# Linear attention on one core: rows 256 to 511 of x transposed by the DMA crossbar instead of TensorE, with the first crossbar transpose issued earlier

## The chip, the core and the metric

The kernel runs on one core of a Trainium2 chip. The core has five engines that run their own instruction streams: TensorE (PE in the profile, with PEld for its weight loads), VectorE (DVE), ScalarE (ACT), GpSimd (POOL) and SyncE (SP). DMAs are issued by an engine's stream, here by SP and ACT, and run on 16 DMA engines that all queues share. The metric is the device time of one execution in microseconds.

## What is computed

One block of linear attention, B=1, S=2048 rows, D=640, 32 heads of 20 columns, all in bf16:

```python
qkv = (x @ wqkv).reshape(B, S, 3, H, Dh) ...      # q, k, v
phi = lambda t: jnp.where(t > 0, t + 1, jnp.exp(t)) + 1e-6
pq, pk = phi(q), phi(k)
kv  = einsum("bhsd,bhse->bhde", pk, v);  z = einsum("bhsd->bhd", pk)
num = einsum("bhqd,bhde->bhqe", pq, kv)
den = einsum("bhqd,bhd->bhq", pq, z)[..., None] + 1e-6
out = (num / den) ... @ wo
```

## The kernel before, in words

x is held twice in SBUF: xn with its rows on the partitions (16 tiles of 128 rows), and xT, its transpose, as five chunks of 128 columns of x. A matmul that computes K for a row tile takes the xT columns of that tile as the stationary operand, so a row tile of K cannot start before its part of xT is there.

The stages follow each other on TensorE in this order:

1. Six warming matmuls on a constant (L269).
2. K: for each row tile st, `k_half(st, 0)` and `k_half(st, 1)` (L273, matmul at L278), five chunks each, ten matmuls a tile, 160 in all. The result lies in two PSUM banks, 2*(st%4) and the next. `k_phi(st)` (L287) then makes phi of it: an Exp on ScalarE (L291) and two operations on VectorE (L293, L296), into pk.
3. P = x^T pk (`p_step`, L305), with xn as the stationary operand, in two halves of the columns. Q tiles (`q_tile`, L331) are put between its steps; they read wqp, a permuted copy of wqn that ScalarE makes at the end of the K stage (L259), and xT.
4. The sums of pk (L350), the small per-head products (L408, L432), the denominators (L454), the spreading of their reciprocals by DMA (L471).
5. The output rows (L487), copied out by ScalarE and VectorE (L509, L512) and stored (L497).

**How xT is filled.** The table XCH (L176) cuts the rows into chunks. The first NPE = 4 chunks, of 128 rows each, are transposed on TensorE: `transpose_x(st, b)` (L189) makes five transposes of 128 by 128 (L194) of the tile xn[st] into PSUM bank b, and two VectorE copies (L199) bring them to xT. The other chunks come straight from DRAM through the DMA crossbar: `load_xT` (L182) issues one transposing DMA each (L184) on SP's queue. Before the change those are seven: one of 128 rows (512 to 639), five of 256 rows, and a last one of 128. `xT_keys` (L205) makes a K tile or a Q tile wait for the chunks that it reads.

**What sets the order.** A planner (`Plan.add`) keeps a list of instructions for each engine in the order in which the code adds them, and works out the semaphore waits from reads and writes. The lists are run in order, so a waiting instruction holds up all that stand behind it on its engine. The first DMAs are issued by `load_wk` (L225): on SP x tile 0, then wk chunk 0, wk chunks 2, then 4, then x tile 3; on ACT x tile 1, wk 1, wk 3, then x tile 2. Behind them on SP stand the crossbar transposes, the first with a wait for wk chunk 4 (L186), and then `load_rest` (L244): wqn, the rest of xn in three loads of four tiles each, wv and wo.

The order on TensorE at the start is written out by hand in a string (L537). `t0` is the transpose of row tile 0, and `k12` is chunk 2 of both halves of K for row tile 1:

```python
order = "t0 t1 k00 k01 k10 k11 k02 k12 k03 k13 t2 k04 k14 t3"
...
transpose_x(st, (st + 2) % 4 + 4)
```

So t0 and t1 use PSUM banks 6 and 7, t2 and t3 banks 4 and 5, which are also the banks of K for row tile 2. After the string follow `k_phi(0)`, `k_phi(1)`, and then, from row tile 2 on, the two halves and phi of each tile.

Of the kernel before, what the change touches and what calls it, by code (L numbers as in the profile page):

```python
# [82 lines left out]
def bass_standalone__linear_attn_block__prompt_kernel(nc, x, wqkv, wo, out):  # L83
    B, S, D = x.shape
# [10 lines left out]
    with contextlib.ExitStack() as ctx:  # L95
        es = ctx.enter_context

        def sb(name, cols, dt=BF16):
            return es(nc.sbuf_tensor(name, [128, cols], dt))

        xT = sb("xT", NC_ * S)
        xn = sb("xn", NT * D)
        wk = sb("wk", NC_ * D)
# [41 lines left out]
        def pool_const():  # L145
# [26 lines left out]
                     0 if lo else DH - 1, 1 if lo else -1, "bm")  # L172


        NPE = 4
        XCH = [(128 * t, 128 * t + 128) for t in range(NPE + 1)] + [  # L176
            (a, min(a + 256, S)) for a in range(128 * NPE + 128, S, 256)]

        def xch_of(row):
            return next(i for i, (a, b) in enumerate(XCH) if a <= row < b)  # L180

        def load_xT():  # L182
            for i, (a, b) in enumerate(XCH[NPE:]):
                P.add("sp", lambda e, a=a, b=b: e.dma_start_transpose(  # L184
                    xT[:, :].rearrange("p (c s) -> p c s", s=S)[:, :, a:b], x[0, a:b, :]),
                    reads=[("wk", 4)] if i == 0 else [],  # L186
                    writes=[("xT", NPE + i)], dma=True)

        def transpose_x(st, b):  # L189
# [15 lines left out]
        def xT_keys(a, b, cs=range(NC_)):  # L205
            keys = []
            for i, (p, q) in enumerate(XCH):
                if p < b and a < q:
                    keys += [("xT", i)] if i >= NPE else sorted(
                        {("xT", i, 0 if c < 2 else 2) for c in cs})  # L210
            return keys

        def w_cols(dst, lo, hi, col, key, eng):
            P.add(eng, lambda e: e.dma_start(
                dst[:, 0:NC_ * D].rearrange("p (c n) -> p c n", n=D)[:, :, lo:hi],
                wqkv[:, col + lo:col + hi].rearrange("(c p) n -> p c n", p=128)),
                writes=[key], dma=True)

        def load_xn(a, b, eng):
            P.add(eng, lambda e: e.dma_start(  # L220
                xn[:, a * D:b * D].rearrange("p (t n) -> p t n", n=D),
                x[0, 128 * a:128 * b, :].rearrange("(t p) n -> p t n", p=128)),
                writes=[("xn", t) for t in range(a, b)], dma=True)

        def load_wk():  # L225
            tl = mybir.InstLoadActFuncSet(
                name=nc.get_next_instruction_name(),
                act_func_set_id=ACT_TABLE_SET_LN_EXP, ins=[], outs=[])
            P.add("act", lambda e: e.add_instruction(tl), writes=["table"])
            for eng, what in (("sp", "x01 w01 w23 w45 x34"), ("act", "x12 w12 w34 x23")):  # L230
                for k in what.split():
                    a, b = int(k[1]), int(k[2])
                    if k[0] == "x":
                        load_xn(a, b, eng)
                    else:
                        P.add(eng, lambda e, a=a, b=b: e.dma_start(
                            wk[:, a * D:b * D].rearrange("p (c n) -> p c n", n=D),
                            wqkv[128 * a:128 * b, D:2 * D].rearrange("(c p) n -> p c n", p=128)),
                            writes=[("wk", c) for c in range(a, b)], dma=True)
# [3 lines left out]

        def load_rest():  # L244
            w_cols(wqn, 0, D, 0, "wqn", "sp")
            for a, b in ((4, 8), (8, 12), (12, 16)):
                load_xn(a, b, "sp")
            w_cols(wv, 0, D, 2 * D, "wv", "sp")
            P.add("sp", lambda e: e.dma_start(
                wog[0:GW, 0:5 * D].rearrange("p (g n) -> p g n", n=D),  # L250
                wo[0:5 * GW, :].rearrange("(g p) n -> p g n", p=GW)),
                writes=["wog"], dma=True)
            P.add("sp", lambda e: e.dma_start(
                wog[0:gsz[5], 5 * D:6 * D], wo[5 * GW:D, :]), writes=["wog5"], dma=True)
# [12 lines left out]
        def warm(*cols):  # L267
            for n in cols:
                P.add("pe", lambda e, n=n: e.matmul(  # L269
                    bank(4, n), one[:, 0:128], one[:, 0:n], start=True, stop=True),  # L270
                    writes=[("bank", 4)])
# [259 lines left out]

        pool_const()
        load_wk()
        load_xT()
        load_rest()
        warm(512, 512, 512, 512, 512, 512)
        order = "t0 t1 k00 k01 k10 k11 k02 k12 k03 k13 t2 k04 k14 t3"  # L537
        for k in order.split():
            st = int(k[1])
            if k[0] == "t":  # L540
# [131 lines left out]
```

## Time and profile before

| what | us |
|---|---|
| median of 3 runs (lowest, highest) | 101.67 (101.2, 102.3) |
| the profiled execution | 101.73 |
| its span from the first to the last instruction | 100.0 |
| TensorE matmuls busy | 96.8 |
| VectorE busy | 69.2 |
| ScalarE busy | 43.3 |
| GpSimd busy | 3.3 |

The times that follow are counted from the span's start. In rows of a timeline, and of the chain that ended last, the first number is the start and the second the duration, or for several merged instructions the busy time, of the group; a note in brackets says how long the engine sat idle before it and what ended that. A DMA row gives the queue that issued it (SPq, ACTq), the size, and the time from issue to landing. A row of windows gives a stretch of time, its length, the busy time and count of PE, PEld, DVE, ACT and POOL, then the granted TensorE clock, the busy share of the DMA engines and the rate of data that they moved.

### The profile page before, as it was taken

The page shows a single profiled execution, that of the slowest core. Times are in us where ns is not written, and L with a number is a line of the kernel's source. Part 1 is how long each engine was busy: PE and PEld are TensorE (multiplying, and loading weights), DVE is VectorE, ACT ScalarE, POOL GpSimd, SP SyncE. Part 2 cuts the span into 40 slices and gives each one's busy share as a digit, 9 for nine tenths or more (in the row PEclk, how much of TensorE's full clock was granted, in tenths as well). Part 3 has the DMA queues.
Part 4 walks back from the last instruction along what each step waited for, and adds up shares of the span by engine and source line. Part 5 has one row for each costly group of instructions (what it writes and reads, how often), then busy time and mean ns, then how long its engine had stood idle before and what let it go on. Part 6 is the DMA issues. An engine that isn't in the chain of part 4 may idle for free.

```text
span 100.0 us, 1793 instructions
## 1 busy us (share of the span) xinstructions
PE 96.8 (97%) x697; PEld 63.0 (63%) x703; DVE 69.2 (69%) x140; ACT 43.3 (43%) x76; POOL 3.3 (3%) x15
## 2 busy tenths in 40 slices
PE   6999999999999999999999999999999999999992
PEld 2556777777777565656667565756446677777771
DVE  0217988888889379799996445758899759853331
ACT  5005554445697220462132227398954523333322
POOL 6600000000000000000000000000000000000000
PEclk9999999999999999999999999999999999999999
DMA  2963999699999900000000000014440324523333
GB/s 56 308 226 71 185 205 137 132 236 377 371 365 289 191 14 0 0 3 0 7 0 0 0 0 0 25 34 123 120 136 1 117 70 153 213 95 120 131 131 131
DMA packets 17076, 11.93 MB, mean 119 GB/s; under 512 B 8749, under 2 KB 17069, under 8 KB 17069
## 3 DMA queue, kind: packets, MB, share of 16 engines
q1 hardware_dynamic: 16349, 11.14, 42.9%
q10 hardware_dynamic: 720, 0.70, 2.1%
q8 instruction: 5, 0.08, 0.3%
q14 instruction: 2, 0.02, 0.1%
HBM read 5.90 MB, written 2.62 MB: 85 GB/s over the span
## 4 chain that ended last, share of the span: by engine, by line
PE 91%; DVE 4%; ACT 2%; issue 1%
PE ps L278 22%; PE ps L487 22%; PE ps L305 22%; PE ps L331 16%; PE ps L269 3%; DVE pq L344 2%; PE ps L194 2%; PE ps L408 2%; PE ps L454 1%; ACT eq L339 1%; DVE pq L479 1%; PE ps L432 1%; DVE eq L341 1%; ACT w2g L436 1%; DVE osb L512 0%
## 5 line engine op out<-in xcount | busy, mean ns | idle before, releaser
L305 PE MATMUL ps<-pk,xn 128*128 128x320 bf16 x160 | 23.5, 299 | 0.0
L331 PE MATMUL ps<-xT,wqp 128*128 128x512 bf16 x94 | 23.1, 379 | 0.3
L278 PE MATMUL ps<-wk,xT 128*128 128x320 bf16 x160 | 22.8, 302 | 0.0
L487 PE MATMUL ps<-w2p,pq 128*128 128x320 bf16 (+1 forms) x165 | 22.1, 295 | 0.1
L339 ACT ACTIVATE eq<-ps 128x512 bf16<-128x512 f32 x20 | 12.0, 599 | 21.2 <-PE ps L331 20.7
L305 PEld LDWEIGHTS ps<-pk,xn 128*128 128x128 bf16 x160 | 15.6, 98 | 7.4 <-DVE pt L320 0.2
L487 PEld LDWEIGHTS ps<-w2p,pq 128*128 128x128 bf16 x165 | 15.8, 98 | 6.6 <-DVE pq L479 0.6
L278 PEld LDWEIGHTS ps<-wk,xT 128*128 128x128 bf16 x160 | 15.4, 99 | 6.6 <-DMA wk<-in_wqkv_dram 0.4
L291 ACT ACTIVATE ek<-ps 128x640 bf16<-128x640 f32 x16 | 11.2, 704 | 14.7 <-PE ps L278 14.7
L331 PEld LDWEIGHTS ps<-xT,wqp 128*128 128x128 bf16 x100 | 9.7, 97 | 9.0
L344 DVE SCALAR_TENSOR_TENSOR pq<-ps,eq 128x512 bf16<-128x512 f32 x20 | 13.8, 692 | 0.7
L296 DVE SCALAR_TENSOR_TENSOR pk<-ps,ek 128x640 bf16<-128x640 f32 x16 | 13.2, 825 | 0.5
L512 DVE CAST osb<-ps 128x320 bf16<-128x320 f32 (+1 forms) x16 | 7.7, 479 | 8.3 <-PE ps L487 8.2
L509 ACT CAST osb<-ps 128x320 bf16<-128x320 f32 (+1 forms) x17 | 7.0, 417 | 13.4 <-PE ps L487 12.1
L341 DVE TENSOR_SCALAR eq<-eq 128x512 bf16<-128x512 bf16 x20 | 5.8, 292 | 9.8 <-ACT eq L339 9.7
L479 DVE TENSOR_TENSOR pq<-pq,rd 128x512 bf16<-128x512 bf16 x20 | 7.7, 416 | 0.4 <-DMA rd<-rdc 0.4
L293 DVE TENSOR_SCALAR ek<-ek 128x640 bf16<-128x640 bf16 x16 | 5.2, 325 | 2.0 <-ACT ek L291 1.9
L199 DVE COPY xT<-ps 128x256 bf16<-128x256 bf16 (+1 forms) x8 | 2.2, 318 | 6.1 <-PE ps L194 6.1
L350 DVE TENSOR_TENSOR za<-pk 128x1280 f32<-128x1280 bf16 x4 | 5.8, 1481 | 0.0
L350 DVE TENSOR_TENSOR za<-za 128x1280 f32<-128x1280 f32 x3 | 4.4, 1480 | 0.0
L259 ACT COPY wqp<-wqn 128x640 bf16<-128x640 bf16 x5 | 4.3, 939 | 0.0
L436 ACT CAST w2g<-ps 120x640 bf16<-120x640 f32 (+1 forms) x6 | 4.0, 690 | 0.0
(38 smaller groups left out, 33.2 us busy)
## 6 DMA issues: line engine op xcount, KB each, us to landing
out_dram<-osb SPq DMA_DIRECT2D x15, 160.0 KB, 1.8
xn<-in_x_dram SPq DMA_DIRECT2D x3, 640.0 KB, 8.0
wqn<-in_wqkv_dram SPq DMA_DIRECT2D x1, 800.0 KB, 5.6
wv<-in_wqkv_dram SPq DMA_DIRECT2D x1, 800.0 KB, 11.2
wog<-in_wo_dram SPq DMA_DIRECT2D x1, 750.0 KB, 13.5
w2p<-w2g SPq DMA_DIRECT2D x5, 150.0 KB
rd<-rdc SPq DMA_DIRECT2D x8, 64.0 KB, 2.3
wk<-in_wqkv_dram SPq DMA_DIRECT2D x3, 160.0 KB, 4.4
```

Source lines behind the costliest of these rows:

```text
L278: r = e.matmul(bank(b + h, HALF), xT[:, c * S + 128 * st:c * S + 128 * st + 128], wk[:, c * D + HALF * h:c * D + HALF * (h + 1)], start=(c ...
L291: P.add("act", lambda e: e.activation(fold(t[:, :]), two_banks(b), ACTF.Exp), reads=banks + ["table"], writes=[("ek", st % 3)])
L296: P.add("dve", lambda e: e.scalar_tensor_tensor(fold(pk[:, st * D:(st + 1) * D]), two_banks(b), 0.0, fold(t[:, :]), ALU.max, ALU.add), rea ...
L305: r = e.matmul(bank(d, HALF), xn[:, st * D + 128 * d:st * D + 128 * d + 128], pk[:, st * D + HALF * h:st * D + HALF * (h + 1)], start=(st ...
L331: r = e.matmul(bank(b), wqp[:, d * D + 128 * c:d * D + 128 * c + 128], xT[:, d * S + BK * sbk:d * S + BK * (sbk + 1)], start=(d == 0), sto ...
L339: P.add("act", lambda e: e.activation(t[:, :], bank(b), ACTF.Exp), reads=[("bank", b), "table"], writes=[("eq", i)])
L344: P.add("dve", lambda e: e.scalar_tensor_tensor(pq[:, c * S + BK * sbk:c * S + BK * (sbk + 1)], bank(b), 0.0, t[:, :], ALU.max, ALU.add), ...
L350: P.add("dve", lambda e: e.tensor_tensor(d_ap, a, b, ALU.add), reads=ra + rb, writes=[dst])
L479: P.add("dve", lambda e: e.tensor_tensor(v, v, rd[i][:, BK * o:BK * (o + 1)], ALU.mult), reads=[("rd", i, 2 * o), ("rd", i, 2 * o + 1), (" ...
L487: r = e.matmul(bank(b, hi - lo), pq[:, c * S + 128 * st:c * S + 128 * st + 128], w2p[:, c * D + lo:c * D + hi], start=(c == 0), stop=(c == ...
L509: P.add("act", lambda e: e.copy(osb[j][:, lo:hi], bank(b, hi - lo)), reads=[("bank", b)], writes=keys)
L512: P.add("dve", lambda e: e.tensor_copy(osb[j][:, lo:hi], bank(b, hi - lo)), reads=[("bank", b)], writes=keys)
```

## The change

Only row tiles 0 and 1 are still transposed on TensorE. Row tiles 2 and 3 (rows 256 to 511) come by the crossbar, as two chunks of 128 rows; the rows from 512 on are cut into six chunks of 256. There are thus eight transposing DMAs. The first of them waits for x tile 1 and no longer for wk chunk 4. The early loads of x tiles 2 and 3 are taken out; these tiles come with the later loads of xn, which now hold four, five and five tiles. The string of the start loses t2 and t3.

```diff
-        NPE = 4
-        XCH = [(128 * t, 128 * t + 128) for t in range(NPE + 1)] + [
-            (a, min(a + 256, S)) for a in range(128 * NPE + 128, S, 256)]
+        NPE = 2
+        XCH = [(128 * t, 128 * t + 128) for t in range(NPE + 2)] + [
+            (a, min(a + 256, S)) for a in range(128 * NPE + 256, S, 256)]
...
                     xT[:, :].rearrange("p (c s) -> p c s", s=S)[:, :, a:b], x[0, a:b, :]),
-                    reads=[("wk", 4)] if i == 0 else [],
+                    reads=[("xn", 1)] if i == 0 else [],
...
-            for eng, what in (("sp", "x01 w01 w23 w45 x34"), ("act", "x12 w12 w34 x23")):
+            for eng, what in (("sp", "x01 w01 w23 w45"), ("act", "x12 w12 w34")):
...
-            for a, b in ((4, 8), (8, 12), (12, 16)):
+            for a, b in ((2, 6), (6, 11), (11, 16)):
                 load_xn(a, b, "sp")
...
-        order = "t0 t1 k00 k01 k10 k11 k02 k12 k03 k13 t2 k04 k14 t3"
+        order = "t0 t1 k00 k01 k10 k11 k02 k12 k03 k13 k04 k14"
```

## The prediction

> **What bounds the kernel now.** I read the page first, its busy shares and the chain that ended last, then that chain in order of time, then TensorE's timeline of the first 10 us, and last the DMA issues with their landings.
>
> ```profile
> span 100.0 us, 1793 instructions
> PE 96.8 (97%) x697; PEld 63.0 (63%) x703; DVE 69.2 (69%) x140; ACT 43.3 (43%) x76; POOL 3.3 (3%) x15
> ...
> PE 91%; DVE 4%; ACT 2%; issue 1%
> ```
>
> TensorE is busy for nearly the whole span and 91% of the chain, so work taken off it there comes off the time, unless it then waits.
>
> ```profile
> 4.78 2.67 PE ps L278 x16
> 7.45 0.38 PE ps L194 x5
> 7.83 0.54 PE ps L278 x4
> 8.38 0.28 PE ps L194 x5
> 8.66 19.16 PE ps L278 x140
> 27.82 4.75 PE ps L305 x35
> ```
>
> The third and fifth lines from the bottom are t3 and t2; both lie on the chain. Behind them 140 matmuls of K (row tiles 2 to 15) run in one piece into the P stage. 4.75 us for 35 matmuls of 320 columns is 0.136 each, so a row tile of ten takes 1.36.
>
> ```profile
> 4.72 2.73 PE L278 MATMUL ps<-wk,xT 128*128 128x320 bf16 x16
> 7.38 0.45 PE L194 MATMUL ps<-ident,xn 128*128 128x128 bf16 x5
> 7.67 0.71 PE L278 MATMUL ps<-wk,xT 128*128 128x320 bf16 x4
> 8.21 0.44 PE L194 MATMUL ps<-ident,xn 128*128 128x128 bf16 x5
> ...
> 8.49 1.12 PE L278 MATMUL ps<-wk,xT 128*128 128x320 bf16 x6
> ...
> 7.38 0.28 PEld L194 LDWEIGHTS ps<-ident,xn 128*128 128x128 bf16 x5 [0.26 <-DMA xn<-in_x_dram]
> ...
> 9.30 0.11 PEld L278 LDWEIGHTS ps<-wk,xT 128*128 128x128 bf16 x2 [0.30 <-DVE xT L199]
> 7.87 0.55 DVE L199 COPY xT<-ps 128x256 bf16<-128x256 bf16 x2 [2.50 <-PE ps L194]
> 8.70 0.56 DVE L199 COPY xT<-ps 128x256 bf16<-128x256 bf16 x2 [0.27 <-PE ps L194]
> ```
>
> This is the same stretch by TensorE's own records. t2 starts when x tile 2 lands; row tile 2 of K starts at 8.49. Its second half waits at 9.30 for the copies of t3, which hold PSUM bank 5.
>
> **The change, part by part.** *t2 and t3 go.* The 16 matmuls end at 4.72 + 2.73 = 7.45. One takes some 0.30 to drain and the next starts 0.136 after it, so k04 can start at 7.45 - 0.30 + 0.14 = 7.29 if wk chunk 4 is there, and row tile 2 four matmuls later, at 7.83, in place of 8.49: 0.66 us earlier. *The bank 5 stall goes.* The six matmuls from 8.49 take 1.12; without a gap they would take 5 x 0.136 + 0.30 = 0.98. That gives 0.14 more, 0.80 in all. The four VectorE copies (1.1 us) go too; VectorE is 69% busy, so I count them at nothing beyond the stall.
>
> What is late next is the crossbar. Row tiles 2, 3 and 4 are now needed at 7.83, 9.19 and 10.55, and every later tile 1.36 after its neighbour.
>
> ```profile
> 7.13 11.99 SPq L184 DMA_TRANSPOSE xT<-in_x_dram  x7
> 19.17 0.58 SPq L214 DMA_DIRECT2D wqn<-in_wqkv_dram  x1
> ...
> L184 SPq DMA_TRANSPOSE xT<-in_x_dram x1: 1331/1331/1331, 7.1 to 7.1; - x1
> ...
> DMA to landing us min/median/max: 3.0/3.0/3.0
> ...
> L184 SPq DMA_TRANSPOSE xT<-in_x_dram x1: 1372/1372/1372, 8.5 to 8.5; - x1
> ...
> DMA to landing us min/median/max: 4.1/4.1/4.1
> ...
> L184 SPq DMA_TRANSPOSE xT<-in_x_dram x1: 1768/1768/1768, 9.9 to 9.9; - x1
> ...
> DMA to landing us min/median/max: 4.4/4.4/4.4
> ...
> xT<-in_x_dram SPq DMA_TRANSPOSE x1, 6.1
> ```
>
> The four single issues are the first (128 rows), the second and third (256 rows) and the one with the longest landing. SP is held some 1.4 us by an issue at first and 1.7 on the mean (11.99 for 7). Landings are 7.13 + 3.0 = 10.1, then 12.6, then 14.3.
>
> ```profile
> 0.84 0.39 ACTq L220 DMA_DIRECT2D xn<-in_x_dram  x1
> ...
> xn<-in_x_dram ACTq DMA_DIRECT2D x1, 160.0 KB, 2.8
> ...
> 2.67 0.43 SPq L220 DMA_DIRECT2D xn<-in_x_dram  x1
> ...
> xn<-in_x_dram SPq DMA_DIRECT2D x1, 160.0 KB, 4.9
> 5.50:6.00 0.50, 0.50 (x5) 0.37 (x4) 0.00 (x0) 0.00 (x0) 0.00 (x0) 1.00 1.04 369
> 7.00:7.50 0.50, 0.50 (x6) 0.22 (x4) 0.00 (x0) 0.00 (x0) 0.00 (x0) 1.00 0.04 15
> 8.50:9.00 0.50, 0.50 (x7) 0.39 (x5) 0.30 (x2) 0.50 (x2) 0.00 (x0) 1.00 0.73 172
> 9.00:9.50 0.50, 0.50 (x5) 0.16 (x4) 0.48 (x2) 0.44 (x1) 0.00 (x0) 1.00 0.89 153
> 9.50:10.00 0.50, 0.50 (x6) 0.35 (x5) 0.48 (x1) 0.00 (x0) 0.00 (x0) 1.00 0.12 28
> ```
>
> *The new wait on SP.* x tile 1 lands at 0.84 + 2.8 = 3.7, and SP, idle since 3.1, issues the first transpose there: 3.4 us before. Behind it on SP stand only the other transposes and the late loads.
>
> *Row tile 2 by the crossbar.* No transpose ran beside plain loads before, so this price is bounded. From below: issue plus 3.0, landing at 6.7. From above: it starts only when the loads are done, as before, and lands at 10.1. The nearest row is x tile 3, whose place behind wk 4 on SP's queue it takes: that landed at 2.67 + 4.9 = 7.6. The same 160 KB move at about 160 GB/s in a transpose (8.50 to 9.50) and at 369 in loads, 1.0 us against 0.44, so 0.55 more. x tile 2, which shared the engines on ACT's queue, is gone: 0.44 less. A transpose's last data were followed by its landing some 0.55 later (9.55 to 10.1), a load's some 0.4 (its last data by 7.2, x tile 3's landing at 7.6): 0.15 more. Together 7.6 + 0.55 - 0.44 + 0.15 = 7.85, against a need of 7.83. I take that. Row tile 3, queued behind it, lands one transfer later, at 8.85, against 9.19.
>
> *Row tiles 4 and 5, one 256-row chunk.* By issues it starts at 3.7 + 2 x 1.38 = 6.46 and lands 4.1 later, at 10.56, against 10.55. If its data wait for row tile 3's, they start at about 8.3, not at the end of its issue (7.87); the 256-row transpose of before landed 2.7 after the end of its issue (8.5 + 1.37 to 12.6), so 11.0: 0.45 late. Between 0 and 0.45 I take 0.25. *Later chunks:* issued at 7.9 and 9.7, with 4.4 and at most 6.1 they land at 12.3 and 15.8, against 13.3 and 16.0; after that the issues are 1.7 apart and the needs 2.7, so the slack grows.
>
> The Trainium skill, page "VectorE: DVE Perf Modes", section "The three transpose paths", gives 1309 ns for a 128 by 128 transpose by the crossbar and 390 ns for one on TensorE, which speaks against the change: five blocks in a row would be an estimated 6.5 us, row tile 2 would land at 10.2, and the sum by it would be a loss of 1.6 us. The trace does not bear it out as a price per block, since ten blocks landed 4.1 us after their issue, and blocks evidently overlap.
>
> *Moved loads.* Eight issues from 3.7 at these rates (11.99 + 1.4) end at about 17.1, so wqn goes out 2 us earlier than at 19.17.
>
> ```profile
> 19.80 2.07 SPq L220 DMA_DIRECT2D xn<-in_x_dram  x3
> ...
> xn<-in_x_dram SPq DMA_DIRECT2D x3, 640.0 KB, 8.0
> wqn<-in_wqkv_dram SPq DMA_DIRECT2D x1, 800.0 KB, 5.6
> ...
> 27.10 0.92 ACT L259 COPY wqp<-wqn 128x640 bf16<-128x640 bf16 x1
> ```
>
> x tiles 2 to 5 then land near 17.7 + 8.0 = 25.7, and P needs tile 2 two steps (1.4 us) after it starts at 27. wqn lands near 22.7, needed at 26.3. Both cost nothing; the 19 us of K matmuls hide them, and without that cover each would cost its whole landing. The two removed loads save two short issues on engines that idle: nothing. After the K stage nothing in the work changes, so I let the gain pass through to the end; the 1.73 us outside the span stay.
>
> **Sum.** 0.66 + 0.14 - 0.25 = 0.55. From the profiled 101.73 that is 101.2; the median of the runs, 101.67, lies 0.06 lower, within the rounding.
>
> **The rivals.** *The transposes are held until the plain loads have landed* (the change then brings nothing). wk 4 landed just before 7.13; from there row tile 2 needs the part after its issue, 3.0 - 1.33 = 1.7, and lands at 8.8: 0.95 late against the 0.80 saved, +0.15. The 256-row chunk may add up to 0.5 behind it. Time 101.9 (101.5 to 102.4). For it: transposes and loads never overlapped before. Against it: loads from two queues shared the engines at 369 GB/s.
>
> *Slower: an early issue buys nothing, and the transpose runs its full 3.0 us only after the loads.* Row tile 2 lands at 10.1 as before: 2.27 late, net +1.47. Row tile 3 follows 1.4 later, and the 256-row chunk about 2.2 after that (the mean of 2.5 and 1.8 between 10.1, 12.6 and 14.3), at 13.7 against 12.8: 0.9 more. Time 103.2 to 104.1, say 103.5. It decides from row tile 2 landing after 8.65 (0.80 after the need); past 9.65 the loss is over 1%. For it: the only transpose that started a series took 3.0 us for what a load moves in 0.44.
>
> *Blocks serial after all:* row tile 2 at 6.7 but each further 128 rows 3.0 later, row tile 4 at 12.7 against 10.55: 2.1 late, 103.1 and growing. The landings 2.5 and 1.8 us apart for 256 rows speak against it.
>
> *All in time:* nothing late, 100.9, if row tile 2 lands near its lower bound and the chunk by its issues.
>
> **How the numbers follow.** The forecast (0.2 to 0.8 gained, 100.9 to 101.5) gets 0.54, all in time 0.10, held transposes 0.20, full price after the loads 0.13, serial blocks 0.03. The predicted time is 101.2. The range is 100.6 to 102.7: below by the all-in-time case less 0.3 for the spread of runs (101.2 to 102.3 before), above by the held case and the same spread; it leaves out the two slow cases, 0.16. About 1% is what a measurement of this kernel can tell from no change. The largest gain that the rows allow is 0.80, under 1%, so faster than that comes only by spread: 0.09. Slower by over 1% is the two slow cases and a little of the held one: 0.18. The rest, 0.73, is within 1%.
>
> **What would show it.** In the changed profile: row tile 2's first matmul near 7.9; first L184 issue near 3.7, landing near 7.9; no copies at L199 after 5.5; a weight load of L278 that waits for the DMA into xT by about 0.25 in all; the first L305 near 27.1 in place of 27.66, and the same 0.55 at the end of the span. The prediction is wrong if the sum of these waits passes 0.8, if wk 4 lands after 7.3 because the transposes delay it, or if the P stage waits for x tile 2.

## The result, and the profile after

| | before | changed |
|---|---|---|
| median of 22 runs (lowest, highest), us | 101.68 (100.88, 102.45) | 100.88 (100.59, 101.72) |
| ratio to before, 95% interval | 1 | 0.9946 (0.9924 to 0.9968) |
| the profiled execution, us | 101.73 | 100.59 |
| its span, us | 100.0 | 99.3 |

The ratio, taken over all 22 executions of each kernel, is worth 0.0054 x 101.68 = 0.55 us (0.33 to 0.77), the gain that was forecast; the two medians differ by 0.80. The profiled execution is the fastest of the 22. It is 1.14 shorter than the one before: 0.68 of that lies in the span (100.0 to 99.3), the rest outside it (1.7 before, 1.3 after), where other profiles differ as much (run 7 has 1.8, run 8 has 1.3).

The page of the changed kernel, busy shares:

```profile
span 99.3 us, 1767 instructions
PE 95.8 (96%) x687; PEld 62.3 (63%) x693; DVE 67.9 (68%) x136; ACT 43.3 (44%) x76; POOL 3.2 (3%) x15
```

Its chain that ended last, in order of time (start, duration, what):

```profile
3.65 1.34 SPq L184
...
5.03 1.26 SPq L184
...
6.33 4.20 DMA xT<-in_x_dram
...
10.57 16.47 PE ps L278 x120
27.05 4.75 PE ps L305 x35
...
74.67 2.88 PE ps L487 x20
```

Before, TensorE was the chain from 0.84 us to 69.0. Now the chain runs over SP: two issues, then the transposing DMA of rows 512 to 767, and K from row tile 4 on starts the moment it lands. The P stage starts at 27.05 in place of 27.82, 0.77 earlier.

TensorE's weight loads of the changed kernel, with its waits:

```profile
4.65 1.49 PEld L278 LDWEIGHTS ps<-wk,xT 128*128 128x128 bf16 x12 [0.19 <-DMA wk<-in_wqkv_dram]
6.46 3.65 PEld L278 LDWEIGHTS ps<-wk,xT 128*128 128x128 bf16 x28 [0.33 <-DMA wk<-in_wqkv_dram]
10.57 3.92 PEld L278 LDWEIGHTS ps<-wk,xT 128*128 128x128 bf16 x30 [0.47 <-DMA xT<-in_x_dram]
```

The 28 from 6.46 are eight for row tiles 0 and 1 and the twenty of row tiles 2 and 3. So row tile 2 starts at 6.46 + 8 x 0.136 = 7.55, row tile 4 could start at 10.27, and it starts at 10.57: 0.30 of stall.

Its issues on SP, and the landings of wk chunk 4 (issued at 2.19) and of the first three transposing DMAs:

```profile
3.65 13.02 SPq L184 DMA_TRANSPOSE xT<-in_x_dram  x8
...
wk<-in_wqkv_dram SPq DMA_DIRECT2D x1, 160.0 KB, 4.4
...
xT<-in_x_dram SPq DMA_TRANSPOSE x1, 3.6
...
xT<-in_x_dram SPq DMA_TRANSPOSE x1, 3.6
...
xT<-in_x_dram SPq DMA_TRANSPOSE x1, 4.2
```

Landings: wk 4 at 6.6 (before: 7.1), row tile 2 at 7.3, row tile 3 at 5.03 + 3.6 = 8.6, row tiles 4 and 5 at 10.5.

**Where the 0.77 comes from.** Row tile 2 starts at 7.55 in place of 8.49, 0.94 earlier: ten transposes at 0.056, 0.56; the wait of t2 for x tile 2 (7.38 against 7.29), 0.09; and chunk 3 of row tiles 0 and 1 starts at 6.46, where before it stood four matmuls behind 6.19, at 6.73: 0.27. These are 0.92 of the 0.94. The 0.27 has two conditions. One is the removal of the x loads: wk chunk 2, for which K waited before, landed at 6.1 then and lands at 5.7 now, so the wait is for chunk 3, which lands at 6.4 in both. The other is that TensorE was at full rate from K's first matmul on (the last section): in the profiles of runs 2 and 4, where the full rate came late, chunk 3 starts at 7.17 and 6.88, no earlier than the 6.73 of before. This part of the 0.77 is thus not in every execution. The bank 5 stall of 0.14 is gone. The new stall takes 0.30 back. 0.94 + 0.14 - 0.30 = 0.78.

The first output matmuls then start at 74.67; in the chain of the kernel before:

```profile
75.29 0.05 issue
75.34 2.89 PE ps L487 x20
```

So 0.67 is left there, and 0.68 at the end of the span. The 0.10 is lost in one place. VectorE's last multiplication ahead of the output starts at 74.95 before and at 74.18 after, still 0.77 earlier; from its end to the first output matmul the changed kernel then takes 0.15 and not 0.05:

```profile
74.18 0.34 DVE pq L479
74.52 0.15 issue
```

Why this step took longer is open.

### The profile page after: what moved, and what is told of

It is laid out like the page before. It is cut to its first block, busy times and chain, and to the rows that moved or that the text cites. A ratio compares the mean times of both kernels' runs of the same rounds, so it can differ in the third digit from the quotient of the medians.

```text
span 99.3 us, 1767 instructions
## 1 busy us (share of the span) xinstructions
PE 95.8 (96%) x687; PEld 62.3 (63%) x693; DVE 67.9 (68%) x136; ACT 43.3 (44%) x76; POOL 3.2 (3%) x15
## 4 chain that ended last, share of the span: by engine, by line
PE 81%; DMA 7%; DVE 4%; SPq 3%; ACT 2%; issue 1%
PE ps L487 22%; PE ps L305 22%; PE ps L278 17%; PE ps L331 16%; DMA xT<-in_x_dram 4%; DMA xn<-in_x_dram 3%; SPq L184 3%; DVE pq L344 2%; PE ps L408 2%; PE ps L454 1%; ACT eq L339 1%; DVE pq L479 1%; PE ps L432 1%; DVE eq L341 1%; ACT w2g L436 1%
## 5 line engine op out<-in xcount | busy, mean ns | idle before, releaser
L278 PE MATMUL ps<-wk,xT 128*128 128x320 bf16 x160 | 22.2, 299 | 0.2
L269 PE MATMUL ps<-const-bfloat16-1.0 128*128 128x512 bf16 x6 | 2.7, 623 | 0.8 <-PEq L657 0.8
## 6 DMA issues: line engine op xcount, KB each, us to landing
xn<-in_x_dram SPq DMA_DIRECT2D x2, 800.0 KB, 10.8
```

Of the source, the lines that this page charges most:

```text
L278: r = e.matmul(bank(b + h, HALF), xT[:, c * S + 128 * st:c * S + 128 * st + 128], wk[:, c * D + HALF * h:c * D + HALF * (h + 1)], start=(c ...
```

## The experiments

Two theories stood at the start. C: the crossbar's chunks land at set times after their issue on SP, and the first issue sets them all. D: the DMA engines are the limit, so an early issue mostly waits behind plain loads. Times are medians, with the ratio to before and its interval.

**1. The old wait put back.**

```diff
-                    reads=[("xn", 1)] if i == 0 else [],
+                    reads=[("wk", 4)] if i == 0 else [],
```

> The changed kernel, but the first transposing DMA waits for wk chunk 4 again, as before the change. Theory C (the landing of the crossbar's chunks, counted from the first issue on SP, sets when K can run): the first issue goes from 3.65 back to 7.1 and all landings go with it, so row tile 2 of K starts at about 10.1 in place of 7.6 and row tile 4 at 13.6 to 14.0 in place of 10.57. That is 3.1 to 3.4 us over the changed kernel, 103.8 to 104.2. Theory D (the DMA engines are the limit, so an early issue mostly waits behind the plain loads): the transposes lose only what they really moved before 7.1, under 1 us, so 101.2 to 101.9.

Measured: 103.29 us, ratio 1.0182 (1.0136 to 1.0229), between the two. TensorE's weight loads, and the landing of the first transposing DMA, issued at 6.06:

```profile
8.98 1.20 PEld L278 LDWEIGHTS ps<-wk,xT 128*128 128x128 bf16 x10 [1.52 <-DMA xT<-in_x_dram]
11.02 1.20 PEld L278 LDWEIGHTS ps<-wk,xT 128*128 128x128 bf16 x10 [0.83 <-DMA xT<-in_x_dram]
12.86 1.61 PEld L278 LDWEIGHTS ps<-wk,xT 128*128 128x128 bf16 x13 [0.65 <-DMA xT<-in_x_dram]
...
xT<-in_x_dram SPq DMA_TRANSPOSE x1, 2.9
```

The first transpose went out at 6.06, not 7.1, because wk 4 landed a microsecond earlier with the two x loads gone. It is 2.41 later than in the changed kernel, row tile 4 starts 12.86 - 10.57 = 2.29 later, and the time is 2.4 us longer. So with the issue where it really came, theory C's rule gives the time of this run; C had only put the issue too late. The early issue is thus needed: without it the change is a loss of 1.8%.

**2. No wait at all before the first transposing DMA.**

```diff
-                    reads=[("xn", 1)] if i == 0 else [],
+                    reads=[],
```

> The changed kernel with no wait before the first transposing DMA, which reads x from DRAM and needs nothing: it can go out at about 2.65, right behind wk chunk 4, 1.0 us before 3.65. Theory C: the 256-row chunk of row tiles 4 and 5 lands at about 9.5 in place of 10.53, before its need at 10.27; the stall of 0.30 us goes, and with it 0.3 of the time: 100.6 against 100.88. Theory D: the data still queue behind the loads and behind each other, the chunk lands at 10.4 or later and the time stays at 100.9; if the transposes even delay the loads of wk, K starts later and the time rises by 0.2 or more.

Measured: 101.02 us, ratio 0.9933 (0.9904 to 0.9962), not to be told from the changed kernel. SP's issues, landings of the first and the third transposing DMA (the third issued at 5.35), and TensorE's weight loads:

```profile
2.67 12.90 SPq L184 DMA_TRANSPOSE xT<-in_x_dram  x8
...
xT<-in_x_dram SPq DMA_TRANSPOSE x1, 4.3
...
xT<-in_x_dram SPq DMA_TRANSPOSE x1, 4.5
...
5.02 9.45 PEld L278 LDWEIGHTS ps<-wk,xT 128*128 128x128 bf16 x67 [0.18 <-issue]
```

Issued 0.98 earlier, the first lands at 7.0, only 0.3 earlier, and the 256-row chunk at 9.8, 0.7 earlier. C had 9.5, D 10.4 or later; neither holds. The last row shows 67 weight loads with no wait for the crossbar: the stall of 0.30 is gone, but this execution began K at 5.02 and not at 4.65, and at half rate (the last section), which hides what that would have brought.

**3. The early loads of x tiles 2 and 3 put back.**

```diff
-... ("sp", "x01 w01 w23 w45"), ("act", "x12 w12 w34") ...
+... ("sp", "x01 w01 w23 w45 x34"), ("act", "x12 w12 w34 x23") ...
-            for a, b in ((2, 6), (6, 11), (11, 16)):
+            for a, b in ((4, 8), (8, 12), (12, 16)):
```

> The changed kernel with the early loads of x tiles 2 and 3 put back where they were (the tiles are not used early; the late loads of xn are again three of four tiles). Theory C: the 256-row chunk is set by its issue at 6.33 and lands at 10.5 again, so row tile 4 starts at 10.6 and the time stays at 100.9, even where row tile 2 starts later, at about 7.9 (its transpose behind x tile 3 on the same queue, some 0.4 to 0.9 later than 7.28). Theory D: everything behind x tile 3 moves by its 0.44 us or more, the chunk lands near 11, and the time is 101.3.

Measured: 101.54 us, ratio 1.0000 (0.9976 to 1.0024). The whole gain is gone. Landings of x tile 3 (issued at 2.66), of the first transpose (3.73) and of the 256-row chunk (6.42), then the weight loads:

```profile
xn<-in_x_dram SPq DMA_DIRECT2D x1, 160.0 KB, 5.2
...
xT<-in_x_dram SPq DMA_TRANSPOSE x1, 4.8
...
xT<-in_x_dram SPq DMA_TRANSPOSE x1, 4.9
...
8.59 2.56 PEld L278 LDWEIGHTS ps<-wk,xT 128*128 128x128 bf16 x20 [0.64 <-DMA xT<-in_x_dram]
11.32 3.24 PEld L278 LDWEIGHTS ps<-wk,xT 128*128 128x128 bf16 x25 [0.17 <-DMA xT<-in_x_dram]
```

The issues stand where they stood, but the first transpose lands at 8.5 and not at 7.3, 0.7 after x tile 3 (7.9), and row tile 4 starts at 11.32, as before the change (11.36, by the same records). Theory C, with landings set by the issues alone, falls.

**4. Rows 512 to 767 in two chunks of 128.**

```diff
-        XCH = [(128 * t, 128 * t + 128) for t in range(NPE + 2)] + [
-            (a, min(a + 256, S)) for a in range(128 * NPE + 256, S, 256)]
+        XCH = [(128 * t, 128 * t + 128) for t in range(NPE + 4)] + [
+            (a, min(a + 256, S)) for a in range(128 * NPE + 512, S, 256)]
```

> The changed kernel with rows 512 to 767 cut into two chunks of 128 rows too (nine transposing DMAs, four of 128 rows first). Theory C: row tile 4 lands 3.6 after an issue at 6.33, at 9.9, and does not wait; row tile 5 lands at about 11.4, need 11.6; but SP's extra issue moves row tiles 6 and 7 to an issue at about 9.0 and a landing at 13.2 to 13.5, need 13.0, so 0.2 to 0.5 of stall comes back there: the time stays within 0.2 of 100.9. Theory D: the data, not the number of issues, set the landings, all later chunks land as before and the 0.30 of stall is gone: 100.6.

Measured: 101.03 us, ratio 0.9938 (0.9914 to 0.9961). The first chunk of 256 rows, now row tiles 6 and 7, was issued at 9.31:

```profile
xT<-in_x_dram SPq DMA_TRANSPOSE x1, 4.4
...
13.77 0.79 PEld L278 LDWEIGHTS ps<-wk,xT 128*128 128x128 bf16 x7 [0.54 <-DMA xT<-in_x_dram]
```

It lands at 13.7, and the stall has moved from row tile 4 to row tile 6. This much of C stands: each further issue holds SP for 1.3 us and moves what is behind it.

**5. The changed kernel again.**

> The changed kernel itself, for a second profile and for the other kernels of this set: 0.9946 of the time before, 101.0 to 101.1 beside 101.57. The first profile of the changed kernel had its TensorE at full rate from 4.4 us on (transposes 0.097 to 0.106 apart, matmuls of K 0.135 apart from the first), the profiles of before and of three experiments only from 5.5 to 6.0 (first matmuls of K 0.22 to 0.27 apart). Where the rate doubles late, row tile 2 of K starts at 7.9 to 8.3 and the 256-row chunk at 10.5 should be hardly late or not late at all; where it doubles early, the stall of 0.3 at row tile 4 comes back.

Measured: 100.76 us, ratio 0.9939 (0.9910 to 0.9968). The gain repeats. TensorE's weight loads:

```profile
6.61 3.65 PEld L278 LDWEIGHTS ps<-wk,xT 128*128 128x128 bf16 x28 [0.41 <-DMA wk<-in_wqkv_dram]
10.64 3.92 PEld L278 LDWEIGHTS ps<-wk,xT 128*128 128x128 bf16 x30 [0.39 <-DMA xT<-in_x_dram]
```

Again TensorE was early at full rate, and the stall at row tile 4 is there: 10.64 - (6.61 + 28 x 0.136) = 0.22. Neither profile of this kernel has a late full rate.

**6. The same loads put back, both on ACT's queue.** The ring order that the prediction used is put to the test: on SP's queue nothing but wk stands ahead of the transposes.

```diff
-... ("act", "x12 w12 w34") ...
+... ("act", "x12 w12 w34 x23 x34") ...
-            for a, b in ((2, 6), (6, 11), (11, 16)):
+            for a, b in ((4, 8), (8, 12), (12, 16)):
```

> The early loads of x tiles 2 and 3 put back, as in the run that brought all of the gain to nothing, but both on ACT's queue, behind wk chunk 3, so that nothing but wk chunk 4 stands ahead of the first transpose on SP's queue. Theory Q (what counts is the place in the same queue: a transpose moves its data only when the loads ahead of it on SP's queue have gone): row tile 2 lands at 7.3 to 7.8 against 8.55, the 256-row chunk at 10.5 to 10.8, and the time is 101.0 to 101.2 beside 101.57. Theory B (what counts is the bytes that share the 16 DMA engines before the transposes are through): the same 320 KB, the same late chunk at 11.2 or later, and the time is that of before, 101.5.

Measured: 101.60 us, ratio 0.9999 (0.9970 to 1.0028). ACT's two x loads and the landing of the second (issued at 2.7), SP's transposes and the first landing, then the weight loads:

```profile
2.22 0.94 ACTq L220 DMA_DIRECT2D xn<-in_x_dram  x2
...
xn<-in_x_dram ACTq DMA_DIRECT2D x1, 160.0 KB, 5.0
...
3.91 13.44 SPq L184 DMA_TRANSPOSE xT<-in_x_dram  x8
...
xT<-in_x_dram SPq DMA_TRANSPOSE x1, 4.5
...
8.40 2.56 PEld L278 LDWEIGHTS ps<-wk,xT 128*128 128x128 bf16 x20 [0.27 <-DMA xT<-in_x_dram]
11.25 3.24 PEld L278 LDWEIGHTS ps<-wk,xT 128*128 128x128 bf16 x25 [0.29 <-DMA xT<-in_x_dram]
```

The x load lands at 7.7 on the other queue, and the transpose at 8.4, 0.7 behind it. Theory B held and Q fell: the place in the queue does not count.

**7. The early issue alone, in the kernel before.** Its first transposing DMA waits for x tile 1; all else is as before.

```diff
-                    reads=[("wk", 4)] if i == 0 else [],
+                    reads=[("xn", 1)] if i == 0 else [],
```

> The kernel before with one part of the change alone: its first transposing DMA waits for x tile 1, not for wk chunk 4, and still four row tiles are transposed on TensorE. Its queue has x tile 3 ahead of the transpose. The transposes that it issues are needed from row tile 4 on, at 11.36, and landed in time before. If an early transpose leaves the plain loads alone, nothing on TensorE's path moves and the time is that of before, within 0.2 us. If it shares the engines with x tile 2 (still in flight until 7.3 on ACT's queue), t2 starts later by up to 0.4 us and the time rises by as much.

Measured: 101.53 us, ratio 1.0005 (0.9972 to 1.0038). Alone it brings nothing. In its profile the transpose (issued at 3.77) and x tile 3 (2.66) landed at 8.5 and 7.9, 0.6 apart.

**8. t2 and t3 in banks 6 and 7, in the kernel before.**

```diff
-                transpose_x(st, (st + 2) % 4 + 4)
+                transpose_x(st, st % 2 + 6)
```

> The kernel before with t2 and t3 in PSUM banks 6 and 7 in place of 4 and 5, nothing else: the stall of 0.14 us in row tile 2, where its second half waits for the copies of t3 out of bank 5, should be gone from the profile, and 0.1 us from the time (too little for the interval). If the stall instead moves to row tile 3, whose columns of xT and whose banks the copies of t3 now both hold until 9.3, the time stays.

Measured: 101.39 us, ratio 0.9992 (0.9960 to 1.0025); as expected the time can't tell it. TensorE's weight loads:

```profile
8.36 2.69 PEld L278 LDWEIGHTS ps<-wk,xT 128*128 128x128 bf16 x21
```

They run through row tiles 2 and 3 with no wait: bank 5 was the cause of that stall, and the stall did not move to row tile 3.

**9. Dead transposes in the changed kernel.** Two times five transposes of x tiles 0 and 1, into banks 4 and 5, with no copies; nobody reads them.

```diff
-        order = "t0 t1 k00 k01 k10 k11 k02 k12 k03 k13 k04 k14"
+        order = "t0 t1 k00 k01 k10 k11 k02 k12 k03 k13 d0 k04 k14 d1"
...
+            elif k[0] == "d":
+                dead_transposes(st, st + 4)
```

> The changed kernel with two times five transposes put back on TensorE where t2 and t3 stood, of x tiles 0 and 1, into banks 4 and 5; no copies follow and nobody reads them. If the work that left TensorE were worth its full 0.56 (ten at 0.056), the time would be 100.88 + 0.56 = 101.4. Theory C with slack: row tile 2 then starts at 8.1 to 8.5 in place of 7.6 to 7.7, but the 256-row chunk at 10.5 is no longer late, so the stall of 0.22 to 0.30 at row tile 4 goes, and the loss is 0.25 to 0.35: 101.2 beside 101.5 for the kernel before.

Measured: 101.24 us, ratio 0.9969 (0.9942 to 0.9996), as expected; against 0.9946 and 0.9939 the loss is 0.23 to 0.31 us, about half of the 0.56 of TensorE work. The intervals overlap, and the whole 0.56 is not excluded either, so the times alone do not show that half is hidden. The weight loads (L210 are the dead ones, and K stands at L288 in this file):

```profile
7.36 0.40 PEld L210 LDWEIGHTS ps<-ident,xn 128*128 128x128 bf16 x5
...
8.18 0.40 PEld L210 LDWEIGHTS ps<-ident,xn 128*128 128x128 bf16 x5
8.54 5.99 PEld L288 LDWEIGHTS ps<-wk,xT 128*128 128x128 bf16 x45
```

K waits nowhere for the crossbar: with this work the chunk is no longer late. TensorE's full rate also came late in this profile, at about 5.8, which takes part of the wait away by itself.

**10. The same dead transposes without the wait of the first transposing DMA** (the edits of 9 and 2 together).

> The same dead transposes in the kernel whose first transposing DMA has no wait. There the chunk landed at 9.8 and nothing on TensorE waited for the crossbar, so the full 0.56 must show against that kernel: ratio 0.9933 + 0.0055 = 0.9988 of the time before. If it is 0.996 or less, row tile 2 was not waiting for TensorE's own work but for the loads of wk.

Measured: 101.28 us, ratio 0.9965 (0.9938 to 0.9993). Both of the stated values lie in the interval, and so the time settles nothing. Its profile adds one thing to run 2. K ran at full rate from its first matmul at 4.61 and waited nowhere for the crossbar; the 256-row chunk landed at 9.9 (issued at 5.35), and without the dead work row tile 4 would have been reached at an estimated 7.97 + 20 x 0.136 - 0.56 = 10.1. So by this estimate the chunk is in time without the wait on SP, even where TensorE is early.

**11. A large plain load beside the first transposes.** x tiles 2 to 5 (640 KB) are loaded early on ACT, and the late load of them on SP goes.

```diff
-... ("act", "x12 w12 w34") ...
+... ("act", "x12 w12 w34 x26") ...
-            for a, b in ((2, 6), (6, 11), (11, 16)):
+            for a, b in ((6, 11), (11, 16)):
```

> The changed kernel with the load of x tiles 2 to 5 (640 KB) moved from its late place on SP to ACT's early queue, behind wk chunk 3, where it is in flight until about 9. In seven profiles so far the first transpose landed 0.63 to 0.76 us after the last plain load ahead of it or beside it, on either queue. Theory H (a transpose does not get through while plain loads are in flight, because it needs all DMA engines at once): row tile 2 lands 0.6 to 0.8 after this load, at 9.3 to 10, and the time is 102.6 or more. Theory S (the queues share the engines in turns, and the transpose's 160 KB are through long before the 640 KB): row tile 2 lands at 7.8 to 8.6, a good while before the load does, and later chunks are late by the shared bytes; time 101.5 to 102.2.

Measured: 102.94 us, ratio 1.0131 (1.0086 to 1.0176), theory H. The large load, its landing, SP's transposes, the first landing, and TensorE's wait:

```profile
2.22 0.46 ACTq L220 DMA_DIRECT2D xn<-in_x_dram  x1
...
xn<-in_x_dram ACTq DMA_DIRECT2D x1, 640.0 KB, 7.1
...
3.72 15.29 SPq L184 DMA_TRANSPOSE xT<-in_x_dram  x8
...
xT<-in_x_dram SPq DMA_TRANSPOSE x1, 6.4
...
10.13 4.46 PEld L278 LDWEIGHTS ps<-wk,xT 128*128 128x128 bf16 x34 [2.00 <-DMA xT<-in_x_dram]
```

The load lands at 9.3 and the 160 KB of the transpose only at 10.1, whereas theory S had it through long before the load. Windows of the same profile (the last two numbers are the busy share of the DMA engines and GB/s):

```profile
8.00:8.50 0.50, 0.47 (x4) 0.10 (x1) 0.00 (x0) 0.27 (x1) 0.00 (x0) 1.00 0.55 144
8.50:9.00 0.50, 0.00 (x0) 0.00 (x0) 0.03 (x1) 0.50 (x2) 0.00 (x0) 1.00 0.46 93
9.00:9.50 0.50, 0.00 (x0) 0.00 (x0) 0.47 (x2) 0.50 (x1) 0.00 (x0) 1.00 1.06 218
```

From 8.0 to 9.0 the engines are about half busy although neither transfer is through, and the rate rises when the load has gone. That fits a transpose that advances only as fast as the engine which is still busiest with the load; it does not prove it.

All runs in which the first transpose was issued with plain loads in flight (run 1 issued it after they had landed; differences are of the unrounded times):

| run | first transpose issued | last plain load lands | the transpose lands | from its issue | from the last load |
|---|---|---|---|---|---|
| changed | 3.65 | 6.6 | 7.3 | 3.6 | 0.7 |
| 2, no wait | 2.67 | 6.3 | 7.0 | 4.3 | 0.7 |
| 3, loads back | 3.73 | 7.9 | 8.5 | 4.8 | 0.7 |
| 4, split | 3.98 | 6.8 | 7.6 | 3.6 | 0.8 |
| 5, again | 3.77 | 6.7 | 7.4 | 3.7 | 0.7 |
| 6, loads on ACT | 3.91 | 7.7 | 8.4 | 4.5 | 0.7 |
| 7, before, early | 3.77 | 7.9 | 8.5 | 4.8 | 0.6 |
| 9, dead transposes | 3.92 | 6.2 | 7.6 | 3.7 | 1.3 |
| 10, dead, no wait | 2.67 | 6.4 | 7.0 | 4.3 | 0.6 |
| 11, large load | 3.72 | 9.3 | 10.1 | 6.4 | 0.8 |

Run 9 does not fit a landing 0.7 after the last load. It shares its 3.7 from the issue with the changed kernel and with runs 4 and 5, though wk chunk 4 landed anywhere from 6.2 to 6.8 in these four. All ten landings come within 0.15 us of the later of two times: 3.6 after the issue, and 0.7 after the last plain load. This was read off afterwards, and only run 9 separates the two for the changed kernel; no run was made to test it.

The packets show what the loads do. A transpose alone moves in packets of under 512 bytes (run 1, 7.25 to 8.5: 672 of 672), plain loads mostly in larger ones. In the changed kernel, from 4.75 to 5.25 and from 5.25 to 5.75:

```profile
DMA packets 167, 0.19 MB, mean 382 GB/s; under 512 B 18, under 2 KB 167, under 8 KB 167
DMA packets 287, 0.11 MB, mean 217 GB/s; under 512 B 248, under 2 KB 287, under 8 KB 287
```

So its data start near 5.25, 1.6 after the issue, against 1.4 in run 1 with nothing else in flight, and before wk chunk 4 has landed: here the loads hardly hold the start back. In run 2 the small packets come up after 5.0 (24 of 171 in the half microsecond before, 174 of 280 in the one after), at least 2.3 after the issue, and in run 11 at 7.0 (3 of 138, then 155 of 264), 3.3 after it. From 7.0 to 9.0 in run 11 both kinds move, 497 small packets of 731: the transpose does advance beside the load, but slowly.

## Why the prediction was right, and where it was not

*TensorE is the chain, and t2 and t3 lie on it: right.* The start of row tile 2 was forecast at 7.83 and came at 7.55 in the changed kernel's profile. The ten transposes and the wait for x tile 2 moved as forecast; the further 0.27, an earlier chunk 3, was not in the sum; it shows where TensorE is early at full rate. In the profiles the parts thus give 0.78 and not the 0.55 of the sum. That the ratio gives 0.55 to the digit is luck: its interval reaches from 0.33 to 0.77.

*The bank 5 stall: right,* by its absence after and by run 8.

*Row tile 2 by the crossbar: right in kind, with the wrong rule.* It was priced at 7.85 by x tile 3's place in SP's queue. It landed at 7.3, and run 6 shows that the queue it stands in is not what counts. Where plain loads were in flight late (runs 3, 6, 7 and 11), or the issue was earliest (2 and 10), it came 0.6 to 0.8 after the last of them, on whichever queue; the rival "held until the plain loads have landed" came near to this. Its price was wrong twice: the rest after the loads is 0.7, not 1.7, and with the x loads gone the last plain load lands at 6.6, not 7.1. In the changed kernel itself the 3.6 from the issue fits as well, and with run 9 better.

*The 256-row chunk: right in size, by luck.* 0.25 late was forecast; two profiles show 0.30 and 0.22. But the forecast landing was about 10.8 and the true one 10.5 to 10.6; the need was earlier by as much, so two errors of 0.2 to 0.3 cancelled.

*The two removed loads at nothing: wrong, and the largest error.* I counted their issues on SP and ACT, and in row tile 2's landing the place of the one and the bytes of the other, but nothing beyond. Runs 3 and 6 put them back, and the gain was 0.00 and 0.01% of the time: row tile 4 started at 11.32 and 11.25 in place of 10.57. Taking the two loads out of the way of the transposes decides between a gain of 0.55 us and none. Their absence also lets wk chunk 2 land 0.5 earlier, from which an early TensorE makes the 0.27. The sum held because the lateness of the chunk, which stood in it, was judged nearly right without the reason.

*The slow rival* (full 3.0 us only after the loads) did not come; run 1 shows what it is like: 2.9 from issue to landing and 1.8% more time. *Blocks serial:* the 256-row chunk took 4.2 from issue; by 1309 ns for a 128 by 128 block in the Trainium skill ("VectorE: DVE Perf Modes", section "The three transpose paths") ten in a row would be an estimated 13 us. The measurement decides: the figure is no price per block in a series.

*The gain passes through to the end: nearly.* 0.77 at the P stage, 0.67 at the output stage in the profiles. The 1.73 outside the span, which was to stay, was 1.3 in the changed profile.

No kernel tried beats the changed one by more than the intervals tell: runs 2 and 4 stand at 0.9933 and 0.9938.

## What to carry to other kernels

A transposing DMA issued early is not early while plain loads are in flight, on its own queue or another. For the 160 KB of this kernel, estimate its landing as the later of 3.6 us after the issue and 0.7 us after the last of these loads lands, and take out of its way every load that can come later. When work on the bounding engine is replaced by a transfer, write down the need and the landing of each chunk, not only of the first; here the third decided. And split what is put back: the dead transposes of run 9 seem to cost half of their own time, with no wait for the late chunk left in the profile, though the intervals leave room for all of it.

## What the runs showed of the hardware that was not expected

TensorE's rate doubles at a point that differs from run to run. Durations (ns, minimum, median, maximum) of K's first matmuls between 4.5 and 5.5 us, first before, then changed:

```profile
L278 PE MATMUL ps<-wk,xT x4: 307/432/474, 4.7 to 5.5; 128*128 128x320 bf16 x4
```

```profile
L278 PE MATMUL ps<-wk,xT x7: 296/298/299, 4.7 to 5.5; 128*128 128x320 bf16 x7
```

The matmul starts then lie 0.22 to 0.27 or 0.135 us apart, and 0.136 in every profile later on. Over the thirteen profiles the change came between 3.6 (run 5) and 6.1 to 6.2 us (runs 2 and 6), while the granted clock stands at 1.00 all the time. The Trainium skill, page "TensorE: Matmul & The Clock Gate", "Part 1: The HAM clock gate (the "warmup" mystery)", has the rule: the clock doubles after a busy window of some 3.4 us, and the window runs freely, so the point depends on where in it the first matmul falls. The traces agree that the point moves, but in run 5 not with the length: the first matmul starts at 0.83 to 0.84 in every profile, so the change came 2.8 to 5.4 us after it, and 2.8 is shorter than such a window. An early point lets TensorE reach the crossbar's chunk sooner and wait for it (10.27 against a landing at 10.53 in the changed kernel); a late one hides the wait. That this makes up part of the spread of the runs (100.59 to 101.72) is a guess that no run here shows.
